# Forward and backward of a gated recurrent-attention layer on one core: projection row loads by SyncE five ahead, weight pieces at half rate, riding rows eight units later

## The chip, the cores and the metric

One core of one Trainium2 chip runs the whole program. A core has a matmul engine (TensorE, PE in the profile, with its weight loads as PEld), a vector engine (VectorE, DVE), a scalar engine (ScalarE, ACT), a general engine (GpSimd, POOL) and SyncE (SP), which only issues transfers. Each engine runs its own queue of instructions in order, and they wait for each other by semaphores. Transfers are carried out by 16 DMA engines; SP, ACT and POOL can issue them. The metric is the time of one execution on the device in microseconds (us).

## The reference

The program computes a forward pass and all its gradients in one launch. Cut to what matters:

```
xn  = layernorm(x)                            # S = 2048 rows, D = 640
s   = A(xn)                                   # memory-augmented attention
g   = silu(B(xn))                             # gated MLP, F = 1728
out = x + s * g
# A: 64 segments of 32 rows; 32 heads of 128; mem has 8 rows
h   = concat(mem, xs)                         # 40 rows of one segment
q, k, v = h @ Wq, h @ Wk, h @ Wv
p   = softmax(mask(q @ k^T * scale))
o   = (p @ v) @ Wo
mem = o[:8];  outs.append(o[8:])              # the next segment's memory
# returned: out and vjp(grad_out) for x, mem0, Wq, Wk, Wv, Wo, w1, w3, w2
```

The memory of a segment is the attention output of the one before, so the forward pass has a chain of 64 steps, and the backward pass a chain of 64 steps in the other direction. All results are bf16.

## The kernel before

The work goes in stages: layer norm and the MLP (`phase12_ln_Bfwd`), projections of all ordinary rows (`phase3_Afwd`), the forward loop over 64 segments (`recurrence`), the backward loop (`phase4_Abwd`), and weight and row gradients (`phase6_Awgrads`, `phase6b_gWo`, `phase5_Bbwd_ln`). The change touches the end of `recurrence` and the start of `phase4_Abwd`, that is, what lies between the two loops.

Each stage is written by hand in the order in which it is to run, and `in_order` (L273) makes every engine follow that written order. Two jobs are woven by Python generators: one job yields after each small piece, and the other calls `next` where a piece may go. So the place of a call in the Python text is its place in the queue of every engine that it uses.

**Units.** Everything in the loops that is not the chain itself is cut into units. A unit is a row tile `tl` (three segments, up to 120 rows of 96 ordinary and 24 memory rows) by a group `qd` of four heads. In the forward part a unit goes through `ld` (L740, rows of q and v to the core, q by SP, in the tail v by POOL), `turn_q` (transposes), `scores`, `soft` (row maximum by VectorE, exponentials by ScalarE, L805), `norm` (L816, P scaled and stored to DRAM as PR), `turn_p` (transposes of P, copy by VectorE) and `pv` (L875, the result stored as OR). The units of the last two row tiles, 13 of them, are left after the loop: the `tail`. In the backward prologue the units of `pro`, 19 of them, go through `ld` (L1272: qv, gor and Pr rows; the memory rows of qv, QVM, by POOL, the rest by SP), `turn` (L1297), `dprob`, `dsoft` and `gmem`. `turn` transposes the v rows, ScalarE copies them to a tile `gvT` (two buffers, L1305 and L1306), POOL stores that as VTD, and then the gradient rows are transposed and copied.

**After the forward loop.** `fill()` (L1016) puts pieces of `work1` (L979) between the steps of the tail units. `work1` has three parts. First, `out_proj` for five blocks of 128 rows: each block has 8 items, an item is one group of four heads; its 128 x 512 rows of OR are loaded (L509), transposed by TensorE (L519), copied to `oTm` by VectorE (L520) and multiplied by Wo (L526), and the two halves of the sum end up in `s_tok` and are stored as SR. Loads are issued by the engine `q`, which is `nc.gpsimd`, three items ahead of use. Four slices of the tile `vt`, which the loop no longer needs, serve as `orow` buffers. In between, `wq_turn` transposes Wq. Meanwhile SP loads Wo transposed (WoT, 16 pieces, `w_ld`), a transfer in which the DMA side does the transposing ("crossbar pieces"), and then Wk transposed (WkT, 16 pieces of two heads). Second, eight groups of the gradient GX: `gx_block` (L1058) multiplies a block of GS, loaded transposed into `g0x` by `gx_ld`, by WoT into a bank, VectorE and ScalarE copy the two halves to `g0st` (two buffers), and POOL stores 1024 columns at a time. Third, `out_proj` for the last 64 rows, of which the first loads are issued ahead of the second part.

**The hand-over.** `phase4_Abwd` takes its tiles where the forward stage had its own, so its first instructions wait until the forward stage has given the memory back, which includes its last SR store. VectorE clears some tiles (`gOTs`, `gors`, `gdSs`), and POOL clears `krb`, a tile of 120 x 2 x 2048 bf16 that later holds two extra sets of unit rows (`xb`); the first units' loads come behind.

**The backward prologue.** A loop over `i` runs turn of unit i, dprob and dsoft of unit i-1 and gmem of unit i-2, and between them pieces of `gx_work`, which does the remaining four blocks of GX with two tiles' worth of transposed GS in the space of `vTt`. Into the same loop fall eight loads of WvT (four heads each, at i = 4 to 11, L1459), and at i = 8 `chain_consts` and two calls for the **riding rows**: `ride_ld(T - 1)` loads 96 rows of GS transposed into `gride`, and `ride(T - 1)` has POOL copy every fourth column of it into `gox` (L1127), the tile from which the backward chain starts. Then the loop over 64 segments begins.

Of the kernel before, what the change touches and what calls it, by code (L numbers as in the profile page):

```python
# [16 lines left out]
P = 128  # L17
# [477 lines left out]
def out_proj(k, Wo, x0, x1, acc, bank, orow, oTs, stok, q, done):  # L495

    nc = k.nc
    items = [(x, min(P, x1 - x), qd) for x in range(x0, x1, P) for qd in range(8)]

    def ld(i):  # L500
        if i >= len(items):
            return
        x, w, qd = items[i]
        a = 0
        while a < w:
            tl, r = divmod(x + a, 96)
            n = min(96 - r, w - a)
            assert tl < k.NTL - 2 or (tl, qd) in done
            q.dma_start(orow[i % len(orow)][a:a + n, :], k.OR[120 * tl + r:120 * tl + r + n, 512 * qd:512 * qd + 512])  # L509
            a += n  # L510

    def turn(i):
        if i >= len(items):
            return
        x, w, qd = items[i]
        r = orow[i % len(orow)]
        pt = bank(w)
        for j in range(4):
            nc.tensor.transpose(pt[:, j, :], r[0:w, j * P:(j + 1) * P], k.ident[0:w, 0:w])  # L519
        nc.vector.tensor_copy(oTs[i % 2][:, :, 0:w], pt)  # L520

    def mm(i, j0, j1):
        x, w, qd = items[i]
        for j in range(j0, j1):
            for h in range(2):
                nc.tensor.matmul(acc[h][0:w, 0:320], oTs[i % 2][:, j, 0:w], Wo[:, 4 * qd + j, 320 * h:320 * h + 320],  # L526
                                 start=(qd == 0 and j == 0), stop=(qd == 7 and j == 3))

    for i in range(3):
        ld(i)  # L530
    yield
    turn(0)
    for i, (x, w, qd) in enumerate(items):
        ld(i + 3)
        turn(i + 1)
        mm(i, 0, 2)
        yield
        mm(i, 2, 4)
        if qd == 7:
            t = stok()  # L540
            for h in range(2):
                k.copy(t[0:w, 320 * h:320 * h + 320], acc[h][0:w, 0:320], eng='vs'[h])
            q.dma_start(k.SR[x:x + w, :], t[0:w, :])
        yield


def recurrence(k, W0, W4, Wv, Wk_, Wq, Wo, kTs, vt, hxs, qTs, xPs, PTs, oTm):
    nc, tc = k.nc, k.tc
    D, DC, S, H, HD, T = k.D, k.DC, k.S, k.H, k.HD, k.T
    with tc.tile_pool(name="achain", bufs=1) as ch, \  # L550
# [161 lines left out]
        def w_ld(n):  # L712
            for _ in range(n):
                if wfetch:
                    turned_load(k, *wfetch.pop(0))
# [253 lines left out]

        bA, bB, bC = [b_[:] for b_ in (bA, bB, bC)]  # L970
        orow = [vt[:, 512 * i:512 * i + 512] for i in range(4)]
        oTs = [oTm[:].rearrange("p a b -> p (a b)")[:, 512 * i:512 * i + 512].rearrange("p (a b) -> p a b", b=P) for i in range(2)]
        stok = lambda: ch.tile([P, D], BF16, name="s_tok", tag="oride")
        obank = lambda w: ps.tile([P, 4, w], BF16, name="opt", tag="x", bufs=5)
# [4 lines left out]
        def work1():  # L979
            w_alloc("q")  # L980
            o = op(X0, X1)
            next(o)
            yield
            g0 = []

            def g_ld(i):
                xs = ch.tile([P, DC, P], BF16, name="g0x", tag=("fup", "oride")[i])
                gx_ld(k, xs, *k.GXB[i])
                g0.append(xs)
            n = 0  # L990
            for _ in o:
                if n % 2 == 0 and n < 2 * H:
                    wq_turn(n // 2)
                n += 1
                yield
                if n == 2 * H:
                    g_ld(0)
                    while wfetch:
                        w_ld(1)
                    w_alloc("k")  # L1000
                elif n > 2 * H:
                    w_ld(1)
            g_ld(1)
            o = op(X1, S)
            next(o)
            for i, (x0, w) in enumerate(k.GXB[0:2]):
                for cg in range(4):
                    sg = ch.tile([P, 1024], BF16, name="g0st", tag="stg", bufs=2)
                    for b in range(2):
                        gx_block(k, g0[i], sg, (bA, bB)[b], WT["o"], x0, w, cg, b, nc.gpsimd)  # L1010
                        w_ld(1)
                        yield
            for _ in o:
                yield

        def fill(n=1):  # L1016
            for _ in range(n):
# [40 lines left out]
def gx_block(k, xs, sg, pb, WoT, x0, w, cg, b, eng):  # L1058

    c0 = cg * 1024 + b * 512  # L1060
    for dc in range(k.DC):
        k.nc.tensor.matmul(pb[0:w, :], xs[:, dc, 0:w], WoT[:, dc, c0:c0 + 512], start=(dc == 0), stop=(dc == k.DC - 1))
    k.copy(sg[0:w, b * 512:(b + 1) * 512], pb[0:w, :], eng='vs'[b])
    if b == 1:
        eng.dma_start(k.GX0[x0 - k.GB0:x0 - k.GB0 + w, cg * 1024:(cg + 1) * 1024], sg[0:w, :])


def phase4_Abwd(k, out2, W4, WT):
# [20 lines left out]
    with tc.tile_pool(name="gst", bufs=1) as st, tc.tile_pool(name="gchain", bufs=1) as ch, \  # L1089
# [4 lines left out]

        gors = [st.tile([120, 512], BF16, name=f"gor{i}") for i in range(NG)]
        gqvs = [st.tile([120, 2, 512], BF16, name=f"gqv{i}") for i in range(NG)]
        gOTs = [st.tile([P, 4, P], BF16, name=f"gOT{i}") for i in range(2)]
        vTb = st.tile([P, H, 40], BF16, name="vTt")
        goxs = [st.tile([P, DC, 32], BF16, name=f"gox{i}") for i in range(2)]
        bdm = st.tile([P, 16, 8], BF16, name="bdm")  # L1100
        xpb = st.tile([P, 8, 2, 32], F32, name="xp")
        gPrs = [st.tile([120, 4, P], BF16, name=f"gPr{i}") for i in range(NG)]
        gdSs = [st.tile([120, 4, P], BF16, name=f"gdS{i}") for i in range(2)]
        krb = st.tile([120, 2, 2048], BF16, name="krb")
        bdf = goxs[0][:, 0:4, :].rearrange("p a b -> p (a b)").rearrange("p (a b) -> p a b", b=8)
        b16 = st.tile([P, 16], F32, name="b16")
        for tt in gOTs + gors + gdSs:
            nc.vector.memset(tt[:], 0.0)
        bA, bB, bC = [psm.tile([P, 512], F32, name=f"gbank{i}") for i in range(3)]
# [310 lines left out]
            nc.sync.dma_start(k.m_rows(k.GWO, t).rearrange("r (c d) -> (r c) d", d=160),  # L1420
                              goxs[t % 2][0:32].rearrange("p a b -> p (a b)"))

        nc.gpsimd.memset(krb[:], 0.0)
        xb = krb
        gx = vTb[:].rearrange("p h c -> p (h c)").rearrange("p (i a b) -> p i a b", i=2, a=DC)
        xs2 = xpb[:].rearrange("p a b c -> p (a b c)").bitcast(BF16)
# [17 lines left out]
        for _ in range(4):  # L1444
            ld_next()
        next(work)
        for _ in range(2):
            ld_next()
        for i in range(len(pro) + 2):
            for f, o in ((turn, 0), (dprob, 1), (dsoft, 1), (gmem, 2)):  # L1450
                if 0 <= i - o < len(pro):
                    f(*pro[i - o])
                if f is not dsoft and not (f is dprob and i % 3):
                    next(work, None)
            if 0 <= i - 2 and (i - 2 + 6 < len(pro) or i >= len(pro) - 2):
                ld_next()
            if 4 <= i < 12:
                h0 = 4 * (i - 4)
                nc.sync.dma_start(WvT[:, h0:h0 + 4, :], k.WVT[:, h0:h0 + 4, :])  # L1459
            if i == 8:  # L1460
                chain_consts()
                ride_ld(T - 1)
                ride(T - 1)
            if i == len(pro):
                for _ in work:
                    pass
                loads(T - 1)
                load_xp(T - 1)
# [786 lines left out]
```

## Time and profile before

| | us |
|---|---|
| runs, median of three | 4761.68 (4761.62, 4761.68, 4773.38) |
| the profiled execution | 4766.39 |
| its span, first to last instruction | 4764.5 |
| TensorE busy | 4452.5 (93%), 64223 matmuls |
| VectorE busy | 2245.4 (47%) |
| GpSimd busy | 2152.3 (45%) |
| ScalarE busy | 1587.8 (33%) |

The mean granted clock of TensorE is 0.979. The program reads 472.66 MB and writes 310.33 MB. Busy time doesn't count the instructions that issue transfers by SP, waits, or branches. In the tables of groups a line stands for one place in the code, one operation and one pair of tiles, for instance

```profile
L873 POOL DMA_DIRECT2D OR<-xv x163 | 89.9, 551 | 364.7 <-ACT xv L92 340.3
L1307 POOL DMA_DIRECT2D VTD<-gvT x176 | 129.9, 745 | 224.5 <-ACT gvT L1306 197.1
```

To be read as: POOL issued 163 stores of `xv` to OR, 89.9 us busy in all and 551 ns each, and stood idle for 364.7 us ahead of them, of which 340.3 ended with ScalarE's copy at L92. The second line is the store of `gvT` to VTD, 176 times. Tile names are those of the code. A wait, in the listings of waits, is told as who waited, at which instruction, for whom and for which tile, then the total of such waits in us, their number and the longest.

### The profile page before, as it was taken

What the parts mean: (1) busy time and instruction counts of PE and PEld (TensorE: products, weight loads), DVE (VectorE), ACT (ScalarE), POOL (GpSimd) and SP (SyncE); (2) the same over time, 40 slices, a digit from 0 to 9 for tenths busy, and PEclk for the clock granted to TensorE, in tenths of its full rate; (3) what the DMA queues carried; (4) which work ended last, traced back from release to release, by engine and by line L of the source; (5) the groups of instructions that cost most, each with busy time, mean ns of one, the idle gap of its engine ahead of it and who ended that gap; (6) DMA issues with size and microseconds to landing.
All of it is one profiled execution on the core that took longest, in us unless ns stands there. A gap on an engine that the chain in (4) does not pass through costs nothing. (4 is left out here: it accounts for less than half of the span.)

```text
span 4764.5 us, 159990 instructions
## 1 busy us (share of the span) xinstructions
PE 4452.5 (93%) x64223; PEld 2829.8 (59%) x64504; DVE 2245.4 (47%) x7154; ACT 1587.8 (33%) x4360; POOL 2152.3 (45%) x3625
## 2 busy tenths in 40 slices
PE   8998999999999777999999998899999999999999
PEld 4544555555555544666666665666667666666675
DVE  8734666666666424555555553332234322311460
ACT  5432555555544423333333332332233322300000
POOL 6532555555555543445444443553345533411340
PEclk9998999999999988999999999999999999999999
DMA  8773665665555567777777774844355443669783
GB/s 265 234 242 107 178 180 172 180 179 175 179 169 167 151 133 222 203 217 211 218 206 208 205 211 120 203 137 120 106 147 160 133 117 109 186 201 218 157 183 98
DMA packets 972135, 834.80 MB, mean 175 GB/s; under 512 B 518546, under 2 KB 853398, under 8 KB 969432
## 3 DMA queue, kind: packets, MB, share of 16 engines
q1 hardware_dynamic: 757551, 543.98, 41.0%
q0 software_dynamic: 133392, 234.80, 16.6%
q10 hardware_dynamic: 80451, 45.78, 3.8%
q8 instruction: 509, 8.34, 0.7%
q14 instruction: 232, 1.90, 0.1%
HBM read 472.66 MB, written 310.33 MB: 164 GB/s over the span
## 5 line engine op out<-in xcount | busy, mean ns | idle before, releaser
L1629 PE MATMUL wg<-gr,hr 128*128 128x512 bf16 x2352 | 519.1, 379 | 2.5
L1610 PE MATMUL g<-w,ghacc 128*128 128x320 bf16 x3072 | 460.3, 300 | 1.1 <-ACT ghacc L92 0.4
L1629 PEld LDWEIGHTS <-hr 128*128 128x128 bf16 x2400 | 233.8, 98 | 279.0
L1610 PEld LDWEIGHTS <-ghacc 128*128 128x128 bf16 x3072 | 288.7, 98 | 104.9 <-ACT ghacc L92 2.5
L306 PEld LDWEIGHTS <-hx 128*32 128x32 bf16 x7680 | 177.8, 97 | 174.2 <-issue 12.5
L90 DVE CAST wgo<-wg 128x512 bf16<-128x512 f32 x72 | 49.8, 692 | 471.2 <-PE wg L1629 471.2
L90 DVE CAST stg<-bank 128x512 bf16<-128x512 f32 x256 | 177.0, 692 | 168.4 <-PE bank L306 154.3
L873 POOL DMA_DIRECT2D OR<-xv x163 | 89.9, 551 | 364.7 <-ACT xv L92 340.3
L1575 POOL DMA_DIRECT2D GSP<-grs x48 | 25.7, 549 | 473.0 <-ACT grs L1567 472.2
L92 ACT COPY ghacc<-t6g 128x768 bf16<-128x768 bf16 (+1 forms) x176 | 137.1, 779 | 300.7 <-PE t6g L1592 296.1
L1307 POOL DMA_DIRECT2D VTD<-gvT x176 | 129.9, 745 | 224.5 <-ACT gvT L1306 197.1
L325 PEld LDWEIGHTS <-gkv 128*8 128x8 bf16 x8192 | 179.9, 87 | 83.6 <-DVE gkv L1179 2.7
L825 POOL TENSOR_TENSOR xP<-xP,xrz 120x480 bf16<-120x480 bf16 x163 | 161.3, 990 | 76.4 <-DVE xrz L824 47.5
L805 ACT ACTIVATE xP<-xsp,xnm 120x120 bf16<-120x120 f32 (+1 forms) x540 | 186.1, 373 | 21.8 <-DVE xnm L787 19.0
L1616 DVE TENSOR_TENSOR ghacc<-ghacc,g 128x320 f32<-128x320 f32 x192 | 93.5, 487 | 209.0 <-PE g L1610 209.0
L92 ACT CAST wgo<-wg 128x512 bf16<-128x512 f32 x48 | 28.1, 585 | 479.8 <-PE wg L1629 407.0
L1336 DVE SCALAR_TENSOR_TENSOR gdS<-gdp,Dx,gPr 120x120 bf16<-120x120 f32 (+1 forms) x680 | 182.9, 331 | 0.0
L1354 POOL DMA_DIRECT2D GXP<-gks x157 | 91.4, 582 | 196.2 <-ACT gks L1352 187.5
L325 PE MATMUL gbank<-WvT,gkv 128*8 128x320 bf16 x4096 | 174.0, 315 | 0.2 <-DVE gkv L1179 0.2
L325 PE MATMUL bank<-Wo,oTm 128*32 128x320 bf16 x4032 | 154.8, 308 | 18.6 <-DVE oTm L677 18.6
L306 PE MATMUL bank<-Wq,hx 128*32 128x512 bf16 x2560 | 163.3, 384 | 5.4 <-DVE stg L90 5.4
L325 PE MATMUL gbank<-WkT,gkv 128*8 128x320 bf16 x4096 | 162.2, 299 | 3.0 <-DVE gkv L1179 1.8
(364 smaller groups left out, 10918.4 us busy)
## 6 DMA issues: line engine op xcount, KB each, us to landing
QVS<-stg SPq DMA_DIRECT2D x128, 256.0 KB
gqv<-QVS SPq DMA_DIRECT2D x108, 192.0 KB
vTt<-VTD SPq DMA_DIRECT2D x64, 320.0 KB
PR<-xP POOLq DMA_DIRECT2D x168, 120.0 KB, 3.1
VTD<-gvT POOLq DMA_DIRECT2D x168, 120.0 KB, 3.8
DSR<-gdS POOLq DMA_DIRECT2D x168, 120.0 KB, 3.0
dS<-DSR SPq DMA_DIRECT2D x168, 120.0 KB
P<-PR SPq DMA_DIRECT2D x168, 120.0 KB
```

What stands on the lines that cost most here:

```text
L90: return nc.vector.tensor_copy(out, in_)
L92: return nc.scalar.copy(out, in_)
L306: k.nc.tensor.matmul(bank[32 * g:32 * g + 32, :], x[:, dc, :], W[:, dc, c0:c0 + 512], start=(dc == 0), stop=(dc == k.DC - 1), tile_positio ...
L325: k.nc.tensor.matmul(pm[p0:p0 + nq, 0:320], x[:, h, :], W[:, h, 320 * b:320 * b + 320], start=(first and i == 0), stop=(last and i == 15), ...
L805: nc.scalar.activation(Pb[0:n, j, 0:n], sp[0:n, j, :], ACT.Exp, bias=nmx[0:n, j:j + 1], scale=k.scale, accum_out=Z[0:n, j:j + 1])
L825: eng.tensor_tensor(Pb[0:n, :, 0:n], Pb[0:n, :, 0:n], bc_last(rz[0:n], n), ALU.mult)
L1307: nc.gpsimd.dma_start(k.VTD[tl][:, :, h0:h0 + 4, :], vTq[:])
L1336: nc.vector.scalar_tensor_tensor(dS[0:n, j, 0:n], dp[0:n, j, :], Dx[0:n, j:j + 1], Pr[0:n, j, 0:n], op0=ALU.subtract, op1=ALU.mult)
L1354: (nc.sync if (tl, qd) in pro else nc.gpsimd).dma_start(k.GXP[tl, :, qd, 0:ns], ks[:].rearrange("p s i h m -> p s i (h m)"))
L1610: nc.tensor.matmul(pg[:], ring[:, i, j, r0:r0 + P], Ws[qd][i][:, j, 320 * h:320 * h + 320], start=(i == 0 and j == 0), stop=(i == 2 and j ...
L1616: nc.vector.tensor_tensor(a, a, pg[:], ALU.add)
L1629: nc.tensor.matmul(pw[:], hr[:, tl, dc * P:(dc + 1) * P], grs[i][:, tl, :], start=(tl == 0), stop=(tl == NF - 1))
```

## The change

- `out_proj`: the row loads are issued by SP (`nc.sync`) and no longer by `q`; SR is still stored by `q`, POOL. Five items are loaded ahead, where it was three, and `orow` gets two further buffers, from the pool that held the tag `kr` in the loop: six in all.
- `work1`: the transposing load of the first gradient block, `g_ld(0)`, is called at n = 40 where it was n = 64. The WkT pieces are asked for at every second step behind n = 64, and in the second part at every second `gx_block`, where it was at every one. So eight pieces go out in the first part and eight in the second. GX is stored there by ScalarE (`nc.scalar`), where it was POOL.
- `phase4_Abwd`: the tiles are allotted in another order; `krb` is cleared by VectorE, behind the loads of the first four units, and no longer by POOL ahead of everything; WvT comes in 16 pieces of two heads at i = 3 to 18; `ride(T - 1)` is called at i = 16, while `ride_ld(T - 1)` stays at i = 8.

No matmul is added or taken away.

```diff
@@ -506,7 +506,7 @@
             tl, r = divmod(x + a, 96)
             n = min(96 - r, w - a)
             assert tl < k.NTL - 2 or (tl, qd) in done
-            q.dma_start(orow[i % len(orow)][a:a + n, :], k.OR[120 * tl + r:120 * tl + r + n, 512 * qd:512 * qd + 512])
+            nc.sync.dma_start(orow[i % len(orow)][a:a + n, :], k.OR[120 * tl + r:120 * tl + r + n, 512 * qd:512 * qd + 512])
             a += n
 
     def turn(i):
@@ -526,12 +526,12 @@
                 nc.tensor.matmul(acc[h][0:w, 0:320], oTs[i % 2][:, j, 0:w], Wo[:, 4 * qd + j, 320 * h:320 * h + 320],
                                  start=(qd == 0 and j == 0), stop=(qd == 7 and j == 3))
 
-    for i in range(3):
+    for i in range(5):
         ld(i)
     yield
     turn(0)
     for i, (x, w, qd) in enumerate(items):
-        ld(i + 3)
+        ld(i + 5)
         turn(i + 1)
         mm(i, 0, 2)
         yield
@@ -969,6 +969,7 @@
 
         bA, bB, bC = [b_[:] for b_ in (bA, bB, bC)]
         orow = [vt[:, 512 * i:512 * i + 512] for i in range(4)]
+        orow += [fl.tile([P, 512], BF16, name="orow", tag="kr", bufs=2)[:] for _ in range(2)]
         oTs = [oTm[:].rearrange("p a b -> p (a b)")[:, 512 * i:512 * i + 512].rearrange("p (a b) -> p a b", b=P) for i in range(2)]
         stok = lambda: ch.tile([P, D], BF16, name="s_tok", tag="oride")
         obank = lambda w: ps.tile([P, 4, w], BF16, name="opt", tag="x", bufs=5)
@@ -993,12 +994,13 @@
                     wq_turn(n // 2)
                 n += 1
                 yield
+                if n == 40:
+                    g_ld(0)
                 if n == 2 * H:
-                    g_ld(0)
                     while wfetch:
                         w_ld(1)
                     w_alloc("k")
-                elif n > 2 * H:
+                elif n > 2 * H and n % 2 == 0:
                     w_ld(1)
             g_ld(1)
             o = op(X1, S)
@@ -1007,11 +1009,14 @@
                 for cg in range(4):
                     sg = ch.tile([P, 1024], BF16, name="g0st", tag="stg", bufs=2)
                     for b in range(2):
-                        gx_block(k, g0[i], sg, (bA, bB)[b], WT["o"], x0, w, cg, b, nc.gpsimd)
-                        w_ld(1)
+                        gx_block(k, g0[i], sg, (bA, bB)[b], WT["o"], x0, w, cg, b, nc.scalar)
+                        if b == 0:
+                            w_ld(1)
                         yield
             for _ in o:
                 yield
+            while wfetch:
+                w_ld(1)
 
         def fill(n=1):
             for _ in range(n):
@@ -1094,16 +1099,16 @@
 
         gors = [st.tile([120, 512], BF16, name=f"gor{i}") for i in range(NG)]
         gqvs = [st.tile([120, 2, 512], BF16, name=f"gqv{i}") for i in range(NG)]
+        vTb = st.tile([P, H, 40], BF16, name="vTt")
+        bdm = st.tile([P, 16, 8], BF16, name="bdm")
+        goxs = [st.tile([P, DC, 32], BF16, name=f"gox{i}") for i in range(2)]
+        b16 = st.tile([P, 16], F32, name="b16")
+        xpb = st.tile([P, 8, 2, 32], F32, name="xp")
+        gdSs = [st.tile([120, 4, P], BF16, name=f"gdS{i}") for i in range(2)]
         gOTs = [st.tile([P, 4, P], BF16, name=f"gOT{i}") for i in range(2)]
-        vTb = st.tile([P, H, 40], BF16, name="vTt")
-        goxs = [st.tile([P, DC, 32], BF16, name=f"gox{i}") for i in range(2)]
-        bdm = st.tile([P, 16, 8], BF16, name="bdm")
-        xpb = st.tile([P, 8, 2, 32], F32, name="xp")
         gPrs = [st.tile([120, 4, P], BF16, name=f"gPr{i}") for i in range(NG)]
-        gdSs = [st.tile([120, 4, P], BF16, name=f"gdS{i}") for i in range(2)]
         krb = st.tile([120, 2, 2048], BF16, name="krb")
         bdf = goxs[0][:, 0:4, :].rearrange("p a b -> p (a b)").rearrange("p (a b) -> p a b", b=8)
-        b16 = st.tile([P, 16], F32, name="b16")
         for tt in gOTs + gors + gdSs:
             nc.vector.memset(tt[:], 0.0)
         bA, bB, bC = [psm.tile([P, 512], F32, name=f"gbank{i}") for i in range(3)]
@@ -1420,7 +1425,6 @@
             nc.sync.dma_start(k.m_rows(k.GWO, t).rearrange("r (c d) -> (r c) d", d=160),
                               goxs[t % 2][0:32].rearrange("p a b -> p (a b)"))
 
-        nc.gpsimd.memset(krb[:], 0.0)
         xb = krb
         gx = vTb[:].rearrange("p h c -> p (h c)").rearrange("p (i a b) -> p i a b", i=2, a=DC)
         xs2 = xpb[:].rearrange("p a b c -> p (a b c)").bitcast(BF16)
@@ -1444,6 +1448,7 @@
         for _ in range(4):
             ld_next()
         next(work)
+        nc.vector.memset(krb[:], 0.0)
         for _ in range(2):
             ld_next()
         for i in range(len(pro) + 2):
@@ -1454,12 +1459,13 @@
                     next(work, None)
             if 0 <= i - 2 and (i - 2 + 6 < len(pro) or i >= len(pro) - 2):
                 ld_next()
-            if 4 <= i < 12:
-                h0 = 4 * (i - 4)
-                nc.sync.dma_start(WvT[:, h0:h0 + 4, :], k.WVT[:, h0:h0 + 4, :])
+            if 3 <= i < 19:
+                h0 = 2 * (i - 3)
+                nc.sync.dma_start(WvT[:, h0:h0 + 2, :], k.WVT[:, h0:h0 + 2, :])
             if i == 8:
                 chain_consts()
                 ride_ld(T - 1)
+            if i == 16:
                 ride(T - 1)
             if i == len(pro):
                 for _ in work:
```

## The prediction

> **What bounds the kernel now.** I read the 40-slice part of the page first, to see where the kernel is not held by TensorE.
>
> ```profile
> PE   8998999999999777999999998899999999999999
> PEclk9998999999999988999999999999999999999999
> DMA  8773665665555567777777774844355443669783
> ```
>
> A slice is 119.1 us. TensorE is at 90% nearly everywhere, but three slices in a row, from 1548 to 1906 us, stand at 7 and two of them have a lower granted clock. This is the stretch between the forward loop and the backward loop, and every edit lies in it. The timeline of TensorE gives its stages, so I asked for busy times in those stretches:
>
> ```profile
> core 0: us, PE busy (x) PEld busy (x) DVE busy (x) ACT busy (x) POOL busy (x), PEclk, DMA share, GB/s
> 1606.80:1614.08 7.28, 0.01 (x1) 0.03 (x1) 0.36 (x2) 0.69 (x2) 6.28 (x12) 0.50 0.94 231
> 1614.08:1729.00 114.92, 88.16 (x922) 62.96 (x924) 39.97 (x119) 46.12 (x160) 61.20 (x119) 0.95 0.68 143
> 1729.00:1770.30 41.30, 33.47 (x175) 17.75 (x174) 7.85 (x17) 4.67 (x8) 12.67 (x25) 0.83 0.54 125
> 1770.30:1784.06 13.76, 0.42 (x9) 0.46 (x10) 2.56 (x9) 1.06 (x4) 7.91 (x9) 0.68 0.31 81
> 1784.06:1829.20 45.14, 41.27 (x359) 21.66 (x365) 20.26 (x123) 16.50 (x59) 14.29 (x27) 0.91 0.71 218
> 1829.20:1868.50 39.30, 22.51 (x246) 16.30 (x243) 21.30 (x124) 13.86 (x48) 16.92 (x27) 0.73 0.93 274
> ```
>
> I call them **a** (the first projection load), **b** (five blocks of output projection, woven with the last forward units), **c** (gradient blocks and the last projection block), **d** (the hand-over), **e** (the backward prologue, its two rows together). The reader is to see 75.8 us of 261.7 without a matmul, the half clock in a, c and e, and that only the last row has its DMA engines nearly full (0.93). Then TensorE's waits, for a and b, for c, and for d and e:
>
> ```profile
> PE opt L519 <- DMA vt<-OR: 27.6, 16, 7.3
> PE bank L526 <- DVE s_tok L90: 3.9, 3, 3.4
> ```
>
> ```profile
> PE bank L1062 <- DVE g0st L90: 4.1, 1, 4.1
> PE bank L1062 <- DMA g0x<-GS: 2.3, 1, 2.3
> ```
>
> ```profile
> PE gvpt L1303 <- DMA gqv<-QVM: 9.2, 1, 9.2
> PE ggpt L1310 <- ACT gvT L1306: 8.2, 2, 7.7
> ...
> PE gbank L1062 <- DMA vTt<-GS: 4.1, 1, 4.1
> PE gbank L1062 <- DVE gstg L90: 3.0, 1, 3.0
> ```
>
> The numbers are total us, times, longest. In b the wait that ends last is the row load, issued by POOL. The 7.7 us of e ends on ScalarE, so I followed it to POOL and ScalarE in 1822 to 1845:
>
> ```profile
> POOL gox L1127 <- DMA gride<-GS: 11.9, 1, 11.9
> ```
>
> ```profile
> ACT gvT L1305 <- DMA VTD<-gvT: 10.1, 1, 10.1
> ```
>
> POOL stood 11.9 us at the copy of the riding rows, which had been asked for just before; the VTD stores behind it were late, the two gvT buffers stayed full, ScalarE stopped, TensorE stopped.
>
> **The change part by part**, against the profiled execution: 4764.5 us span, 4766.4 us for the run. The median of the runs is 4761.7, 0.1% less, and I subtract the same sum from it.
>
> *Rows by SP, five ahead (a and b).* 96 loads leave POOL (median 519 ns each there, 1.9 to 5.1 us to landing) and go to SP, where a load of like size (xq, L265) takes 0.31 to 0.35 us. In a, POOL reaches its first load at 1610.36 and the row lands at 1614.05, 3.7 us later. SP is past its last transposing load at 1608.5; with the same 3.7 us the row is there at 1612.2. **a: 1.9 us less** (ends 0 and 4: behind the four WoT transposes on SP's own queue, or in the shortest landing).
>
> In b there are 27.6 - 7.3 = 20.3 us of row waits in 15 places. They come from POOL's order, not from slow transfers: at 1703 the row loads stand behind the PR store, which waited 5.7 us for ScalarE's exponentials, and TensorE waits 4.1 us. On SP the neighbours are the q loads, which wait for TensorE to free the buffer, up to 8.9 us at a time, and one 1.5 us transposing load per unit. But a q load waits for a transpose that TensorE reaches at the same place in its own order, so SP goes on when TensorE gets there, and it then holds at least four loaded items, of 2.3 to 2.9 us, against 3 to 4 us of landing. So all 20.3 us go. About 2 us more go with the half clock after the 4.1 us gap (a group of four matmuls takes 1.24 us there, 0.71 otherwise).
>
> What is late next is VectorE. It holds from the row maximum to the copy of P: 1637.72 to 1641.35, waiting inside for ScalarE; the oTm copy of the next item stands behind it, and TensorE has about 1.5 us of its own item plus 1 us of the unit to fill with. In the trace of before this shows once, with 3.4 us; elsewhere the row waits hide it. For 13 units I take 0.5 us each, about 6 (ends: 0, and 1 us each, 13). **b: 20.3 + 2 - 6 = 16 us less** (5 to 22).
>
> A rule that speaks against this edit: the Trainium skill, "DMA: Bandwidth & Descriptors", Issuing engines are not separate DMA queues, says that all issuers run on the same 16 engines, so that another issuer saves the issue time only. By it, b gains at most the 0.2 us per load: two loads before each of 15 waits, 6 us. By the row, the engines were 0.68 busy in b and the loads landed in 3 us once issued, while POOL issued them late. I take the row; the rule gives the first rival.
>
> *Half-rate crossbar pieces, first gradient load early, stores by ScalarE (c).* 16 blocks at 1.08 us (at full clock) and 8 items at 1.42 are 28.7 us; the other 12.6 are the waits (4.1, 2.3, 1.1 for a row) and 5.1 us of half clock (10 matmuls in 4.43 us instead of 2.16; the next 40 in 11.41 instead of 8.64). The second gradient load stood behind all 16 WkT pieces:
>
> ```profile
> L270 SPq DMA_TRANSPOSE WkT<-in_A_Wk_dram x16: 1322/1940/3097, 1711.7 to 1741.4; - x16
> ```
>
> (durations in ns, least, median, most). Now 8 are ahead of it, 15.5 us of SP earlier: the 2.3 us go. The store that held g0st was issued 1.1 us after its copy and took 5.9 us among the WkT pieces. ScalarE issues it at once (0.33 us, ScalarE is idle). But nothing slows the second eight: SP runs ahead of TensorE, and they fall into the middle of these blocks, with two staging tiles as before. I leave 4.5 us of short waits, too short to drop the clock. **c: 8 us less** (2 to 12). On SP the last three items' rows are behind these eight; TensorE needs them some 25 us into c, about when they land; cover gone, 3 us.
>
> *Tiles in a new order, krb cleared by VectorE (d).* Every first instruction of the backward stage still waits for the last SR store (issued 1771.23, seen at 1773.4). POOL loses 3.5 us of memset, so the first QVM row comes about 3 us sooner; but then TensorE waits for vTt, whose transposing load SP issues at 1780.14 after twelve loads, as before. **d: 0** (0.5 either way). A rule against it: "SBUF — State Buffer", Who interferes with whom, has VectorE in a two-port mode lock POOL out of writing descriptors. By its list a plain memset isn't such an operation on this chip, and no run here shows one beside POOL's DMAs. Were it one, 4.4 us (memset row: 0.272 us for 512 bytes per partition, krb 16 of these) would put the QVM rows at about 1780.5, still ahead of 1784.06: zero by either.
>
> *WvT in 16 pieces, riding rows eight units later (e).* The 7.7 us go; so does most of 3.0 us, a gstg store caught behind two 640 KB WvT pieces; 1.6 us of half clock after 1840 go too: 12.3. But the DMA engines carry 0.71 x 45.1 + 0.93 x 39.3 = 68.6 us of work in these 84.4 us; in 72.1 they would be at 0.95, and WvT moves into the part with the large units, where VTD stores already hold ScalarE for 0.4 to 2.3 us. I give back 3. **e: 9 us less** (2 to 14).
>
> Sum: 1.9 + 16 + 8 + 0 + 9 = 35, so 4731 for the profiled execution and **4726 us** for the median. TensorE's order of work is the same in both programs, so the loops themselves get 0.
>
> **The rivals.** *Bandwidth, not issue* (chance 0.12): by the rule above b gives 6, c 2, e 3, with a 12 to 13: 4749. For it: shares of 0.9 and more in e and above 1 around 1730. Against: b at 0.68. *VectorE takes the row waits' place* (0.20): 1 us and more per unit, b gives 5: 24 in all, 4738. For it: POOL's and VectorE's waits for ScalarE's exponentials, 22.7 us on VectorE alone. *Everything comes through* (0.15): b 20, c 12, e 14, 48 in all: 4714. *SP becomes the jam* (0.05, slower): row loads stand behind a q load that waits for TensorE, behind a 1.5 to 1.9 us transpose. It decides once that exceeds the lead of five items, 11.5 us; the longest wait, 8.9, with one transpose and two loads makes 11.1. Each unit would then show a whole landing and a transpose, 4.7 us; 13 are 61 instead of 20, and with 19 saved elsewhere the run is 22 us slower: 4783. Against it: SP is freed by TensorE itself.
>
> **The numbers.** The likeliest case has 0.45, by itself 4716 to 4737; 0.03 for what I don't see. Changes under 0.3% (14 us) can't be told from none: 4747 is the border. All of the first, second and third of the better cases lie below it, with some of the bandwidth case: faster 0.86, same 0.09, slower 0.05. The range 4706 to 4750 leaves out about 2 in 10.
>
> **What would show it.** Right: no row waits on TensorE over 1 us after the first; about 98 us for b, 33 for c, 13.8 for d, 75 for e; POOL's stop at L1127 gone. Wrong: row waits that stay with SP's q loads in front (the jam), s_tok or oTm waits that fill b (VectorE), VTD and GX stores landing in over 6 us with shares near 1 in e (bandwidth), d shorter by 3 us (the memset was on the path).

## The result and the profile after

The changed kernel takes 4731.99 us (median of four runs, 4723.40 to 4738.04), the kernel before 4763.22 (four runs, 4761.62 to 4773.38): a ratio of 0.9929, 95% interval 0.9906 to 0.9951, or 31.2 us less. The forecast was 4726 us, 35 us less. Measured again later, the same two kernels differed by 42.9 us (medians of six and of eleven runs, 4724.25 and 4767.10; ratio 0.9916, 0.9901 to 0.9932; after_again below), so the forecast lies between two measurements of the same change. The profiled execution took 4735.54 us, its span is 4733.5, 31.0 less than before. The page's three rows of slices again:

```profile
PE   8998999999999887999999998999999999999999
PEclk9998999999999998999999998999999999999999
DMA  7773565666555578777777774754355543669683
```

A slice is 118.3 us here. Where three slices stood at 7 there are now 8, 8 and 7, and one slice of the three instead of two has the lower clock. The busy times in the five stages, in the columns shown before (us, busy time of TensorE, its weight loads, VectorE, ScalarE, GpSimd; granted clock, DMA share, GB/s):

```profile
1608.22:1613.99 5.77, 0.00 (x0) 0.03 (x1) 0.35 (x2) 0.68 (x2) 3.26 (x5) 0.50 1.01 240
1613.99:1708.36 94.37, 84.81 (x921) 62.12 (x922) 38.89 (x119) 46.00 (x160) 23.55 (x45) 0.95 0.74 166
1708.36:1748.58 40.22, 31.52 (x176) 17.44 (x175) 7.84 (x17) 4.68 (x9) 0.55 (x1) 0.92 0.78 153
1748.58:1760.00 11.42, 0.42 (x9) 0.33 (x8) 4.33 (x10) 1.06 (x4) 4.45 (x8) 0.69 0.26 70
1760.00:1841.73 81.73, 61.47 (x608) 36.55 (x609) 41.62 (x246) 30.22 (x106) 31.16 (x54) 0.81 0.83 248
```

The border between the last two rows is a round number; the stage d really ends at 1761.60, with the first vTt block. So measured by the same events as before (a: last transposes of the loop to the first transposes of rows; b: to the first gradient block; c: to the end of the last projection matmul; d: to the first vTt block; e: to the first block of the backward chain), the stages in us are:

| | a | b | c | d | e | sum |
|---|---|---|---|---|---|---|
| before | 7.3 | 114.7 | 41.6 | 13.8 | 84.4 | 261.7 |
| changed | 5.8 | 94.4 | 40.2 | 13.0 | 80.1 | 233.5 |
| saved | 1.5 | 20.3 | 1.3 | 0.7 | 4.3 | 28.2 |
| forecast | 1.9 | 16 | 8 | 0 | 9 | 35 |

The other 2.8 us of the 31.0 lie outside of the five stages, where no edit is. Over the fourteen profiles of this study the time outside ran from 4484.0 to 4514.9 us, without order by kernel, so single executions are compared by the stages below, and not by the span.

TensorE's waits in the changed kernel, in the same columns as before (total us, times, longest). For b, then for c:

```profile
PE opt L519 <- DMA vt<-OR: 7.4, 2, 5.8
PE bank L526 <- DVE s_tok L90: 4.6, 4, 3.4
PE bank L526 <- DVE oTm L520: 3.0, 5, 0.9
```

```profile
PE bank L1067 <- DVE g0st L90: 4.7, 3, 1.7
PE opt L519 <- DMA orow<-OR: 3.7, 1, 3.7
```

The 5.8 us in the first line are a itself. The row waits of b have thus gone from 20.3 to 1.6 us, and VectorE's share, s_tok and oTm, has grown from 4.2 (3.9 and 0.3) to 7.6. In c the wait for g0x is gone, but g0st has as much as before and a wait of 3.7 us for rows has come. For d and e:

```profile
PE gkp L1353 <- ACT gks L1357: 7.6, 4, 2.8
PE gvpt L1308 <- DMA gqv<-QVM: 6.5, 1, 6.5
PE gbank L1067 <- DMA vTt<-GS: 6.1, 1, 6.1
PE gkp L1353 <- DVE gdS L1341: 3.7, 2, 3.6
PE gvpt L1308 <- ACT gks L1357: 2.6, 1, 2.6
```

The 7.7 us of waiting for gvT are gone, and gks, the tile that ScalarE fills and the GXP store empties, has 7.6 and 2.6.

### The profile page after: what moved, and what is told of

Its sections match the earlier page's. It is cut to its first block, busy times and chain, and to the rows that moved or that the text cites. A ratio compares the mean times of both kernels' runs of the same rounds, so it can differ in the third digit from the quotient of the medians.

```text
span 4733.5 us, 160277 instructions
## 1 busy us (share of the span) xinstructions
PE 4479.4 (95%) x64504; PEld 2827.3 (60%) x64504; DVE 2245.7 (47%) x7155; ACT 1587.4 (34%) x4360; POOL 2096.0 (44%) x3520
## 5 line engine op out<-in xcount | busy, mean ns | idle before, releaser
L245 POOL DMA_DIRECT2D r<-GOS x256 | 145.7, 573 | 42.9 <-issue 10.7
```

The costliest lines, as they stand in the source:

```text
L245: eng.dma_start(d, src if src.shape[0] > 1 else src[0])
```

## The experiments

Each of the twelve kernels was run beside the kernel before on one chip; four chips were used. Their stages, in us, from one profile each:

| kernel | a | b | c | d | e | ratio to before (95%) |
|---|---|---|---|---|---|---|
| rows_sp3 | 5.1 | 104.7 | 36.9 | 13.9 | 84.9 | 0.9940 (0.9921 to 0.9959) |
| rows_pool5 | 7.5 | 99.2 | 38.6 | 13.4 | 81.6 | 0.9947 (0.9926 to 0.9967) |
| rows_both | 5.3 | 97.3 | 43.3 | 13.7 | 85.3 | 0.9929 (0.9908 to 0.9950) |
| gx_pool | 6.1 | 94.7 | 34.2 | 13.5 | 77.1 | 0.9898 (0.9878 to 0.9918) |
| k_late | 6.0 | 93.4 | 33.0 | 14.9 | 78.4 | 0.9908 (0.9892 to 0.9925) |
| krb_pool | 5.0 | 95.3 | 37.5 | 14.1 | 78.4 | 0.9912 (0.9889 to 0.9936) |
| ride8 | 6.1 | 93.8 | 36.7 | 13.4 | 82.8 | 0.9913 (0.9893 to 0.9933) |
| wv8 | 6.2 | 92.9 | 36.3 | 13.4 | 87.7 | 0.9925 (0.9906 to 0.9945) |
| gks3 | 4.9 | 94.6 | 40.1 | 13.3 | 82.2 | 0.9899 (0.9879 to 0.9919) |
| vt_first | 6.6 | 93.1 | 37.4 | 9.4 | 76.5 | 0.9905 (0.9889 to 0.9922) |
| vt_wv | 6.2 | 93.9 | 34.4 | 8.7 | 79.0 | 0.9899 (0.9885 to 0.9914) |
| after_again | 6.4 | 93.5 | 36.3 | 12.8 | 82.3 | 0.9916 (0.9901 to 0.9932) |

The table also says how much one stage varies with the same code. For b the ten profiles with the whole row edit and the half rate lie between 92.9 and 95.3. For c the six with c as changed (the first profile, krb_pool, ride8, wv8, gks3, after_again) lie between 36.3 and 40.2, mean 37.9: the first profile had the longest. For e the five with e as changed (the first profile, gx_pool, k_late, krb_pool, after_again) lie between 77.1 and 82.3, mean 79.3, and the four with e as before between 81.6 and 85.3, mean 84.0. A difference of 3 us in b is thus a finding; in c and e it is not. The kernel before has one profile only. In all twelve rows its median time minus the kernel's own is larger than what the stages save, by 1 to 23 us; where that remainder lies isn't shown.

**Who issues the rows, and how early.** Three kernels built from the one before.

```diff
 rows_sp3
-            q.dma_start(orow[i % len(orow)][a:a + n, :],
+            nc.sync.dma_start(orow[i % len(orow)][a:a + n, :],
 rows_pool5
-    for i in range(3):
+    for i in range(5):
-        ld(i + 3)
+        ld(i + 5)
+        orow += [fl.tile([P, 512], BF16, name="orow", tag="kr", bufs=2)[:] for _ in range(2)]
 rows_both
 both of these
```

> The kernel before with one edit: SyncE issues the row loads of out_proj, still three ahead with four buffers, WkT at full rate. Theory (issue order: the loads were late because GpSimd stood at its stores): a falls to 5.8 us, b loses 12 to 18 of its 20.3 us of row waits up to item 32, but gives some back at its end, where two WkT pieces of 1.9 us stand between the loads of each item: b 98 to 104 us. Rival (depth: five ahead did it): with three ahead b stays above 109. c, d and e stay within 2 us of 41.6, 13.8 and 84.4.

> The kernel before with one edit: five items ahead and six buffers, GpSimd still the issuer. Theory (issue order): a stays at 7.3 us or grows by two more loads issued first (none of it on the path); the lead of five items, 11.5 us, covers GpSimd's longest stop of 5.7 us in part, but its queue is the same: b 104 to 110 us. Rival (depth): b falls to 94 to 98 us with the issuer unchanged.

> The kernel before with SyncE as the issuer and five ahead, everything else as before, so 16 WkT pieces are asked for in the last eight items of b. Theory: a 5.8 us; b is short up to item 32, then SyncE needs 2 x 1.9 + 2 x 0.6 = 5 us an item where TensorE takes 2.9, which uses up the lead and costs 5 to 10 us: b 99 to 105 us, that is, the half rate is a condition of the row edit and not an edit of c. Rival (the two are independent): b 94 to 96 us as in the changed kernel. c between 35 and 42 us; d and e as before within 2 us.

Measured: b 104.7, 99.2 and 97.3. The first is just above the 98 to 104 of its theory, the other two lie between theory and rival. In the first the row waits of b are 13.7 - 5.1 = 8.6 us. Some of them are in the timeline of TensorE (start, length, instruction, in brackets the idle time before it and who ended it):

```profile
1698.64 0.40 PE L519 MATMUL opt<-ident,vt 128*128 128x128 bf16 x4 [3.55 <-DMA vt<-OR]
1701.98 0.59 PE L519 MATMUL opt<-ident,vt 128*128 128x128 bf16 x4 [0.66 <-DMA vt<-OR]
1706.72 0.59 PE L519 MATMUL opt<-ident,vt 128*128 128x128 bf16 x4 [2.02 <-DMA vt<-OR]
1711.08 0.38 PE L519 MATMUL opt<-ident,vt 128*128 128x128 bf16 x4 [1.18 <-DMA vt<-OR]
```

These four are 7.4 of the 8.6 us, and all come after 1689.9, the time at which SyncE issued its first WkT piece. Up to there, with three items ahead, two waits of 1.2 us together were left. So up to there the late loads did come from GpSimd's order, and a quicker transfer or a longer lead was not needed for that. But a longer lead does it as well: with GpSimd as the issuer and five ahead 5.7 us of row waits are left in b, the longest of 3.2, and b lies between what the theory of the issuer (104 to 110) and its rival (94 to 98) allowed, nearer to the rival. The two edits cover for each other, 10.0 us of b for the one, 15.4 for the other and 17.4 for both.

The end of rows_both shows what the half rate is for. SyncE's queue:

```profile
1685.67 1.71 SPq L509 DMA_DIRECT2D vt<-OR  x2
1687.47 3.41 SPq L270 DMA_TRANSPOSE WkT<-in_A_Wk_dram  x2
1690.93 1.23 SPq L509 DMA_DIRECT2D vt<-OR  x2
1692.21 3.44 SPq L270 DMA_TRANSPOSE WkT<-in_A_Wk_dram  x2
1695.77 1.15 SPq L509 DMA_DIRECT2D vt<-OR  x2
1696.96 23.56 SPq L270 DMA_TRANSPOSE WkT<-in_A_Wk_dram  x12
1720.75 1.19 SPq L270 DMA_TRANSPOSE g0x<-GS  x1
1722.03 3.31 SPq L509 DMA_DIRECT2D vt<-OR  x7
```

Two pieces and two loads take SyncE 4.8 to 5.3 us an item, as expected, and the twelve pieces in a row hold the second gradient block's load until 1720.75. TensorE then waits 10.0 us in one place for g0x, and c is 43.3 us. From there to the changed kernel b loses another 3.3 us (97.3 to 94.0, the mean of the ten) and c 5.4 (43.3 to 37.9, the mean of the six; the earlier first load and the stores by ScalarE are in this too). So the half rate adds to the row edit, but is no condition of it: at the full rate b gives back 3.3 us, less than the 5 to 10 expected, and 17.4 us stay.

**What holds c.** Two kernels built from the changed one.

```diff
 gx_pool
-                        gx_block(k, g0[i], sg, (bA, bB)[b], WT["o"], x0, w, cg, b, nc.scalar)
+                        gx_block(k, g0[i], sg, (bA, bB)[b], WT["o"], x0, w, cg, b, nc.gpsimd)
 k_late
-                        if b == 0:
-                            w_ld(1)
                         yield
```

> The changed kernel with one edit undone: the GX stores of c issued by GpSimd again. Theory (a store by ScalarE waits for a transfer that SyncE issued about eight earlier, and that stands behind WkT pieces: three stores go out 2 to 3 us after their copy): TensorE's waits for g0st fall from 4.7 to under 2.5 us and c from 40.2 to 37 to 39 us; the wait of 3.7 us for the orow rows stays. Rival (the prediction: ScalarE's issue is the quicker one): g0st waits grow, c 41 to 44 us. a, b, d, e as in the changed kernel.

> The changed kernel, but the second eight WkT pieces are asked for behind the last row loads of c and not between its gradient blocks. Theory (the pieces in c hold up the rows of the last three items and the GX stores): the row wait of 3.7 us, the half clock behind it of about 3 us and most of the 4.7 us of g0st waits go: c 30 to 34 us against 40.2; the pieces then run into the hand-over, and d, to the first vTt block, may grow by 0 to 3 us. Rival (two staging tiles and a store's landing bound c whatever SyncE does): c 37 us or more.

k_late gives c = 33.0 us, below all six profiles of the changed c, and two waits over 0.3 us are left in it:

```profile
PE bank L1065 <- DVE g0st L90: 2.3, 1, 2.3
PE bank L1065 <- DVE s_tok L90: 0.4, 1, 0.4
```

So by this profile it was the eight pieces between the gradient blocks that held c up. A part comes back in d, which is 14.9 us with the pieces in front of the hand-over, 1.7 more than the changed kernel's mean of 13.2. How they do it stands in the queues of SyncE and ScalarE in the changed kernel:

```profile
1714.15 5.06 SPq L509 DMA_DIRECT2D vt<-OR  x8
1719.26 0.88 SPq L509 DMA_DIRECT2D orow<-OR  x2
1720.18 14.83 SPq L270 DMA_TRANSPOSE WkT<-in_A_Wk_dram  x8
1735.06 1.07 SPq L509 DMA_DIRECT2D orow<-OR  x2
```

```profile
1715.94 0.58 ACT L92 CAST g0st<-bank 128x512 bf16<-128x512 f32 x1 [2.48 <-DMA GX<-g0st]
1718.87 0.34 ACTq L1070 DMA_DIRECT2D GX<-g0st  x1
...
1731.03 0.58 ACT L92 CAST g0st<-bank 96x512 bf16<-96x512 f32 x1 [2.56 <-PE bank L1067]
1734.85 0.31 ACTq L1070 DMA_DIRECT2D GX<-g0st  x1
```

The next rows go out 14.9 us after these eight pieces began; TensorE's wait of 3.7 us ended when they had landed, and the two groups of eight matmuls behind it took 2.34 us each instead of 1.27. In the second fence ScalarE has finished its copy at 1716.52 and issues the store at 1718.87, and later at 1731.61 and 1734.85. VectorE's half of the tile was done by then too, and ScalarE was idle between: by the semaphores in the trace these stores wait, beside the copies, for transfers that SyncE was given a few places earlier (the store of 1718.87 for one of the row loads begun at 1714.15, that of 1734.85 for a WkT piece). With GpSimd as the issuer c is 34.2, with a row wait of 1.1 and g0st at 2.8. The direction is the expected one, the sizes are not: c was to be 37 to 39, g0st under 2.5, and the row wait was to stay at 3.7. Two further kernels with GpSimd's stores had 37.4 and 34.4, a mean of 35.3 for the three against 37.9, and the ranges overlap: that ScalarE's stores cost 2 us or so is likely, and not shown. As gx_pool, with the pieces in place, comes within 1.2 us of k_late, what the pieces cost without ScalarE's stores behind them is open too.

Nor is it shown that the edits of c gain anything there taken together. In rows_sp3 and rows_pool5 the gradient blocks, the pieces between them and GpSimd's stores are as before, and c is 36.9 and 38.6, inside the range of the changed c. The 41.6 of before is a single profile, and rows_both's 43.3 holds the wait of 10.0 us for g0x.

**d.** krb_pool puts the clearing back.

```diff
 krb_pool
+        nc.gpsimd.memset(krb[:], 0.0)
         xb = krb
...
-        nc.vector.memset(krb[:], 0.0)
```

> The changed kernel with krb cleared by GpSimd ahead of its loads again. Prediction: the first QVM rows come 2.7 to 3.5 us later, but the transposing load of vTt ends d, so d from the last projection matmul to the first vTt block stays at 13.0 us (within 1). Rival (the clearing was on the path): d 15 to 16 us.

d is 14.1 us; the six profiles with hand-over and c as changed, or only the store moved, lie between 12.8 and 13.5 (k_late, whose pieces run into d, has 14.9). TensorE waits 9.4 us for the first QVM rows and then 4.2 for vTt; in the changed kernel 6.5 and 6.1:

```profile
PE gvpt L1308 <- DMA gqv<-QVM: 9.4, 1, 9.4
PE gbank L1067 <- DMA vTt<-GS: 4.2, 1, 4.2
```

What the clearing saves on the first wait comes back in the second, but for some 0.8 us by this one profile. The stage is set by SyncE, which has twelve unit loads ahead of vTt, and that was tried directly:

```diff
 vt_first (with the store of gx_pool)
             for i in range(2):
                 gx_ld(k, gx[:, i], *blocks[i])
-            yield
+                yield
...
-        for _ in range(4):
-            ld_next()
         next(work)
+        for _ in range(2):
+            ld_next()
+        next(work)
+        for _ in range(2):
+            ld_next()
```

> The changed kernel with GX stored by GpSimd in c, and the two transposing loads of vTt asked for ahead of the loads of the first and the third unit in place of behind the fourth. Theory (d is set by SyncE's twelve unit loads ahead of vTt): d falls from 13.4 to 8 to 10 us, where the rows of the first unit become the last to arrive; c as in the run with GX by GpSimd, 34 to 36 us. Rival (the landing of the first rows bounds d): d stays above 12 us.

d falls to 9.4 us, as the theory had it; no other kernel but vt_wv, which is built from this one, is below 12.8. (c, at 37.4, is above the 34 to 36 expected.) The first unit's rows are now the last to come, and the wait for vTt is gone from the timeline of TensorE:

```profile
1748.73 0.29 PE L1308 MATMUL gvpt<-ident,gqv 40*128 40x40 bf16 x4 [8.60 <-DMA gqv<-QVS]
1748.95 0.29 PE L1315 MATMUL ggpt<-ident,gor 40*128 40x40 bf16 x4
1749.57 5.41 PE L1067 MATMUL gbank<-WoT,vTt 128*128 128x512 bf16 x14 [0.33 <-issue]
```

**What holds e.** Three kernels built from the changed one.

```diff
 ride8
                 ride_ld(T - 1)      (at i == 8)
-            if i == 16:
                 ride(T - 1)
 wv8
-            if 3 <= i < 19:
-                h0 = 2 * (i - 3)
-                nc.sync.dma_start(WvT[:, h0:h0 + 2, :], k.WVT[:, h0:h0 + 2, :])
+            if 4 <= i < 12:
+                h0 = 4 * (i - 4)
+                nc.sync.dma_start(WvT[:, h0:h0 + 4, :], k.WVT[:, h0:h0 + 4, :])
 gks3
-            ks = fl.tile([P, ns, 2, 4, 8], F32, name="gks", tag="gks", bufs=2)
+            ks = fl.tile([P, ns, 2, 4, 8], F32, name="gks", tag="gks", bufs=3)
```

> The changed kernel with the riding rows copied at i = 8 again, right behind their load; WvT still in 16 pieces. Theory (GpSimd stands at the copy for the load's landing, VTD stores behind it are late, ScalarE and TensorE stop): GpSimd's stop at the copy is back with 5 to 12 us, TensorE shows 5 to 8 us of waits for gvT, and e, from the first vTt block to the first block of the backward chain, is 84 to 89 us against 80.1. Rival (e is held by the DMA engines, so that a stop is made up for by idle engines later): e 79 to 82 us.

> The changed kernel with WvT in eight pieces of four heads at i = 4 to 11 again; the riding rows stay at i = 16. The changed kernel's e was 77.1 to 80.1 us in four profiles, with the riding rows at i = 8 it was 82.8, before 84.4. Theory (the two edits of e add up): e 80 to 83 us, with a gstg or VTD store caught behind two pieces. Rival (the split is worth nothing, the later copy is all): e 77 to 80 us.

> The changed kernel with three buffers for gks where there were two. Theory (with the stop of GpSimd gone, ScalarE's wait for the GXP stores took part of its place: 9.4 us on ScalarE, 7.6 us on TensorE): ScalarE's waits for GXP fall under 3 us and e falls by 2 to 4 us, to 74 to 77. Rival (DMA engines at 0.8 to 0.9 bound e): the waits move to gvT or gdS and e stays at 77 to 80 us.

In gks3 the small tile `b16` also moved into another tile, to make room. ride8 has the stop back, in GpSimd's waits, and its result in TensorE's:

```profile
POOL gox L1132 <- DMA gride<-GS: 9.2, 1, 9.2
```

```profile
PE gkp L1353 <- DVE gdS L1341: 9.2, 6, 2.2
PE gbank L1067 <- DMA vTt<-GS: 6.5, 1, 6.5
PE ggpt L1315 <- ACT gvT L1311: 4.2, 1, 4.2
```

The chain that I had read off the trace of before (the copy stops GpSimd, VTD stores are late, ScalarE's two buffers stay full, TensorE stops) is there again with 4.2 us. But e is 82.8, below the 84 to 89 expected, and the changed kernel run again had 82.3 with the later copy: these profiles don't tell the two apart, and the wait of 4.2 us doesn't show in e. In wv8 the copy is at i = 16, and GpSimd doesn't stop there, yet e is 87.7, longer than any other and than both theory (80 to 83) and rival (77 to 80) had it: gdS has 8.6 us on TensorE, gstg 3.7 and gks 3.7. Of the two edits the split is the one of which a profile shows an effect, 5.4 us above the longest of the five with e as changed, and they don't simply add up.

In gks3 TensorE waits 0.6 us for gks, where the first profile of the changed kernel had 10.2, and 10.8 for gdS; e is 82.2. The changed kernel run again, with two buffers, shows nearly the same list without any help:

```profile
PE gkp L1353 <- DVE gdS L1341: 11.4, 7, 3.6
PE gbank L1067 <- DMA vTt<-GS: 6.0, 1, 6.0
PE gbank L1067 <- DVE gstg L90: 4.2, 2, 2.2
```

So which of gks and gdS is waited for changes from one execution to the next, and the third buffer gained nothing that e shows: the wait for gks was not the cause, only the last to end. The rival was right in that, though e is above its 77 to 80. Its own cause, the DMA engines, is tested next.

**Less traffic late in e, and the changed kernel again.**

```diff
 vt_wv (vt_first, and)
+        for h0 in range(0, 16, 2):
+            nc.sync.dma_start(WvT[:, h0:h0 + 2, :], k.WVT[:, h0:h0 + 2, :])
         for i in range(len(pro) + 2):
...
-            if 3 <= i < 19:
-                h0 = 2 * (i - 3)
+            if 3 <= i < 19 and i % 2:
+                h0 = 16 + i - 3
```

> The kernel of the run with vTt asked for early and GX stored by GpSimd (between the loops 223.0 us, against 233.5 in the profile of the changed kernel), and in addition eight of the 16 WvT pieces ahead of the prologue's first unit, where the DMA engines are at 0.2 to 0.6, and the other eight at every second unit. Theory (e is held by the traffic in its second half): e falls from 76.5 to 70 to 74 us, the waits for GXP and gvT shrink; the run is 10 to 16 us faster than the changed kernel run again beside it. Rival (the early pieces delay the first units' rows): d or the first 15 us of e grow by as much, e 76 to 80 us.

> The changed kernel once more, on the same chip as the kernel above, for its time beside it and for how much one stage varies between two profiles of one kernel. Theory: ratio to before 0.990 to 0.994, a, b, c, d, e within 2 us of 5.8, 94.4, 38, 13.3 and 79; rival (the gain of the first profile was in part the time outside the five stages): between the loops 233 us or more.

The theory failed: e is 79.0, not 70 to 74. This lies in the rival's range of 76 to 80, but the 2.5 us above vt_first's 76.5 are within the spread of e, and d, 8.7, did not grow. The busy times of e in three parts, first vt_first, then vt_wv:

```profile
1749.57:1769.00 19.43, 19.18 (x155) 9.15 (x158) 8.79 (x54) 6.67 (x25) 5.88 (x11) 0.88 0.55 154
1769.00:1800.00 31.00, 27.12 (x271) 16.25 (x274) 17.31 (x98) 13.62 (x46) 14.77 (x27) 1.00 0.99 286
1800.00:1826.04 26.04, 14.32 (x179) 11.34 (x177) 15.59 (x95) 10.30 (x37) 11.24 (x19) 0.60 0.99 320
```

```profile
1746.83:1766.00 19.17, 17.40 (x130) 7.98 (x128) 6.92 (x41) 6.21 (x24) 4.40 (x8) 0.87 0.75 251
1766.00:1800.00 34.00, 31.33 (x315) 18.33 (x314) 18.99 (x112) 14.88 (x50) 17.50 (x31) 1.00 0.94 271
1800.00:1825.78 25.78, 13.39 (x172) 10.55 (x170) 15.65 (x95) 9.81 (x35) 10.43 (x17) 0.62 0.89 282
```

The traffic was moved as meant: 154 to 251 GB/s in the first part, 320 to 282 in the last. TensorE does less in the first part, 130 matmuls where there were 155, as the rival had it. The last part still takes 26 us, at a clock of 0.6, and TensorE's longest total of waits there is again gdS (9.4 us). So the DMA engines' share is high in e, but taking load off them in the last part didn't shorten that part; by one profile of each kernel this speaks against them as what bounds it. What bounds the last 26 us is open; each unit passes TensorE, ScalarE, TensorE, VectorE and TensorE in turn, and GX has no blocks left to fill with, but no run took that apart.

vt_wv has the shortest median of the kernels tried, though by the ratio to before gx_pool and gks3 are level with it: 4717.85 us (five runs, 4716.66 to 4718.23), beside 4724.25 for the changed kernel on the same chip (six runs, 4718.64 to 4737.96) and 4767.10 for the one before. The 6.4 us between the two medians are less than the 10 to 16 expected, and the intervals of their ratios to before overlap, though all its runs are below all of the other's. after_again came out as expected but for e (82.3, where 77 to 81 was expected); its five stages sum to 231.3 us.

## Why the prediction was right, and where not

**The whole.** 35 us were forecast and 31.2 measured, with the median inside the likeliest case's own range. The sum is nearer than its terms: b gave more, c and e less, and that these errors cancelled was luck. The repeat gave 42.9 us, of which the five stages account for 30.4.

**a, 1.9 us.** 1.5 in the first profile; the other nine with the whole row edit and the half rate have 4.9 to 6.6 us for a, before it was 7.3. Right, by the step given. (The prediction's remark that only the last row has its DMA engines nearly full passes over a, whose share is 0.94; no term rests on it.)

**b, 16 us.** 20.3. The row waits went nearly as forecast, from 20.3 to a single one of 1.6, where none over 1 us was to be left. The term that was mis-sized is VectorE's, set at 6 us: s_tok and oTm together grew by 7.6 - 4.2 = 3.4. The other difference is in the half clock: 2 us were forecast, TensorE's busy time fell by 87.91 - 84.81 = 3.1 for the same 921 matmuls (before, with the border of b put at the first gradient block, 1728.75). The idle time fell by the other 17.2. That SyncE would be free when needed held to the end of b with the help of the half rate, worth 3.3 us there; I had charged the WkT pieces to c alone and did not see that, at the full rate, they stand in the same queue as the rows. The rule of the Trainium skill ("DMA: Bandwidth & Descriptors", Issuing engines are not separate DMA queues), by which another issuer saves the issue time only, would have given 6 us by my estimate; 20.3 were measured, and rows_sp3, with nothing else changed, had 10.0. The estimate counts two loads ahead of each wait only: GpSimd's busy time in b fell by 61.20 - 23.55 = 37.7 us, and no run separates that relief from the stops in its queue. Rows ready in 3 us but asked for late were the trouble, as the trace said.

**c, 8 us.** 1.3 in the profile, 3.7 by the mean of six, against one profile of before. The step that failed first is a term set at nothing: "cover gone, 3 us" was named and not charged. In the first profile the row wait is 3.7 us, and TensorE is busy for 31.5 us where the sum at full clock was 28.7; these make 6.5 of the some 7 us by which c exceeds the 33 forecast. In the other five profiles the row wait is 0.4 to 2.5 us. Nor are all short waits "too short to drop the clock": in ride8 ten matmuls behind a wait of 2.17 us for g0st took 3.98 us, where twenty behind one of 1.64 took 4.48. The 4.5 us left for the short waits were right in size (g0st has 3.2 to 5.1 in the six profiles), but not for the reason given: "ScalarE issues it at once (0.33 us, ScalarE is idle)" is wrong, since stores were up to 3.2 us behind their copy with ScalarE idle, waiting for a transfer of SyncE's. With the second eight pieces moved behind the rows, k_late's c is 33.0, of which d gives back 1.7; that this is the 33 that was forecast is chance, for the forecast left the pieces in.

**d, 0.** 0.7 in the profile and 0.5 by the mean of 13.2. Right in the mechanism: the earlier QVM rows for the most part only lengthen the wait for vTt. vt_first confirms what ends d. The case in which VectorE's clearing locks GpSimd out did not show: GpSimd's four QVM issues, from 1752.58 on, ran beside VectorE's smaller memsets (1751.97 to 1754.27) and took 2.23 us, as before, in agreement with the list in the Trainium skill, "SBUF — State Buffer", Who interferes with whom. The large one for krb began at 1754.64, took 1.76 us, where 4.4 had been worked out, and was only partly beside issues, so for it this isn't shown.

**e, 9 us.** 4.3 in the profile, 4.7 between the means (84.0 and 79.3). The step that failed is the give-back: of 12.3 us named I gave back 3, and it was some 8. "The 7.7 us go" is true of that wait, but others came in its place (gks with 10.2 in one profile, gdS with 11.4 in another): TensorE's listed waits in e come to 19.3 us before and 17.7 in the first profile after, and its busy time fell by 2.3. The reason named for the give-back, that e would run into the DMA engines, is open. Their share over the whole of e was 0.84 and not 0.95, but 0.98 and 0.92 in its last 62 us; vt_wv took traffic out of the end of e without gain. What the chain of a unit waits for when gvT is in time should have been named, and was not.

**The rivals.** SyncE as the jam didn't come: its waits for TensorE before q loads were at most 3.5 us in the changed kernel. Rows_both shows its form, though, behind the WkT pieces and not behind q loads. VectorE took 3.4 of the 18.7 us of row waits that went in b, and not the place of most of them. Bandwidth was wrong for b; for e it isn't settled. *Everything comes through* was right in b (20 forecast, 20.3 measured) and wrong in c and e.

## What to carry to other kernels

When loads are late, look at the queue of the engine that issues them before the transfer's length; moving them to another queue and asking for them earlier are two cures for the same delay, and their gains did not add. When a load is moved to a queue, everything else that is asked for there becomes its neighbour: here thinning out the weight pieces was worth 3.3 us in b, and those left in c still cost some 5 us of it by one profile, 3 when what comes back in d is taken off. A long wait in a stage where four engines pass units around can be worth less than its length: price it by the wait that comes next.

## What the runs showed that I had not expected

A store issued by an idle ScalarE went out up to 3.2 us after its data were ready, waiting for a transfer of SyncE's. The same code's c varied between 36.3 and 40.2 us and e between 77.1 and 82.3 from one profile to another, on several chips, while b stayed within 92.9 and 95.3; a verdict on a microsecond or two in c or e takes several profiles.
